# First four units of a fused scan and MLP kernel: memsets moved back, a clip moved forward, weights converted at other places, another rule for warming products

## The chip, the cores and the metric

The kernel runs on one core of one Trainium2 chip. The metric is the time of one execution on the device in microseconds (us); several runs are taken and their median is given. A trace of one profiled execution goes with it; its times count from the start of its span.

## What is computed

Three stages follow each other. The first is a state-space scan over x (4 batches, 8 heads, 768 steps, 32 wide) with decays a and matrices B and C of 16 states:

```python
log_a = np.log(np.clip(a, 1e-06, 1.0))
for c in range(nc):                    # chunks of the sequence
    L = np.exp(cum[..., :, None] - cum[..., None, :]) * causal
    M = np.einsum('bhin,bhjn->bhij', Cc, Bc) * L
    y = M @ xc + (Cc @ state) * np.exp(cum)
    state = decay_full * state + sum_j(Bc x xc * decay_from_j)
```

The second takes its result as 3072 tokens of 256 numbers, norms them (`x / sqrt(mean(x*x) + 1e-6) * g`) and runs a gated MLP, `silu(xn @ w_gate) * (xn @ w_val) @ w_out`, 1536 wide. The third is `softplus(x @ w_in) @ w_out`, 2048 wide.

## The kernel before

The scan is cut into 24 units of 128 steps of one batch, and the MLPs into six blocks of four units (512 tokens). Units 0 to 3 form block 0, and nothing of the MLPs can run until they are done and normed. Matrix products are made in three passes of fp32r parts: every operand has a high part (a copy on ScalarE, ACT) and a low part (a subtraction on VectorE, DVE).

**A unit.** For units 0 to 3 TensorE (PE) spreads the decays over 128 partitions (`spread0`, `spread1`, L539 to L551) into PSUM, DVE runs a scan over each half (L552), PE multiplies C by B (`scores`, L577 to L587), DVE multiplies scores by decays (`decay`, L601), POOL or DVE scales B (`scale`, L572), and PE makes the unit's products (L613 to L626). Then ACT squares them (L648) and applies the gains (L651), PE sums the squares (`msum`), ACT takes the mean (L727), POOL the root (`power`, L729), PE spreads it (`rspread`), DVE multiplies (`norm`, L750), and high and low parts are made (`high` on ACT L347, `low` on POOL or DVE L354). PE has four PSUM buffers `p`, one of which belongs to the warming products, and two each of `a` and `t`.

**The start.** The decays of units 0 to 3 come in by two small loads into `st`, are clipped on DVE (`clip4`, L894), copied on ACT (L897), subtracted on DVE (L898), and only then can be spread. POOL clears `st` first, later the tiles `zz` (used by the weights) and `cz` (used from unit 8 on). The decays of all units are loaded into a tile `s`, clipped on DVE (`clip_all`, L902 and a memset, L903) and stored to `a_clip` in DRAM (L910), from which the units behind the fourth read them back; POOL clips the tile once more in place (L909), DVE makes running products of it (L931) and they too are stored.

**A weight.** Each of 34 chunks (512 KB) is loaded into one of three buffers `wr` (L428), then ACT converts 16 bits of it into `zz` (L436), DVE shifts and joins (L439), ACT makes the high part (L443) and DVE the low part (L445). For the first two chunks `FIRST` gives the places of these four steps.

**The order.** All instructions are issued in an order that a planner makes when the kernel is built. An operation recorded while `plan.now` has a value is a lead operation: on its engine, lead operations run in the order of these values, which `LEAD` and `FIRST` give for the first four units (0 is the first scan; negative values around `LOADS` belong to the start). A first pass of the planner places the lead operations alone and notes a time for each, `due`. The second pass places all: other operations go in between, those of lower `rank` first, where they don't push the next lead operation of their engine more than `SLIP` (100 ns) past its due time. The planner reckons 300 ns for a hand-off between engines, a clock of PE of its own (`clock`), and lets POOL hold the port that it shares with DVE's operations marked `port`.

**Warming products.** Up to 200 products of a constant (`filler`, 512 columns each, rank `SPARE`) serve to keep PE at work; what is not placed when the last lead operation is out is dropped. Before the change they go by the rule of the other operations: the whole of one has to end by the next lead operation's due time of the first pass, plus `SLIP`.

Of the kernel before, what the change touches and what calls it, by code (L numbers as in the profile page):

```python
# [36 lines left out]

LOADS = -50.0

FIRST = [(12.5, 14.8, 17.0, 17.3), (13.0, 15.4, 17.8, 20.4)]  # L40

LEAD = dict(
    spread0=(-0.6, 0.0, 2.6, 6.1), spread1=(-0.4, 1.5, 3.7, 9.6), scores=(-0.2, 4.9, 8.4, 12.1), products=(6.0, 9.5, 13.5, 15.0),
    msum=(7.9, 11.1, 15.3, 16.9), rspread=(10.6, 13.2, 17.9, 18.9),
    scan0=(0.0, 2.28, 5.75, 9.3), scan1=(1.14, 4.6, 8.1, 11.95), decay0=(3.4, 6.9, 10.4, 13.3), decay1=(4.0, 7.5, 11.0, 13.9),
    scale=(2.6, 6.0, 9.6, 13.1), norm=(11.6, 14.5, 18.3, 19.4),
    square=(7.3, 10.8, 14.5, 16.3), gains=(7.6, 11.1, 14.9, 16.6), mean=(8.7, 11.9, 16.8, 17.65), state=(8.8, 12.0, 17.7, 19.0),
    power=(8.9, 12.2, 17.3, 18.3), high=(12.2, 15.1, 18.9, 19.9), low=(12.9, 15.6, 18.8, 20.0))

W_LEAD, T0, U_LEAD, U_GAP, U_GAP0, U1, U1_GAP, B_LEAD, EPI = 50, 50, 115, 8, 4, 10, 14, 50, 40  # L50
# [1 line left out]
SLIP = 100  # L52
# [25 lines left out]
class Plan:  # L78
# [58 lines left out]
    def run(self, which, due, times, warm=False):  # L137

        ops, seq = self.ops, self.seq
# [35 lines left out]
        cand = {e: set() for e in engines}  # L175
        free = {e: 0.0 for e in engines}
        port = 0.0
        queues, served = ("sp", "actq"), 0.0
        ticks = {}

        def enter(i):
            for e in ops[i][0]:
                cand[e].add(i)

        def start(i, e):
            t = max(ready[i], free[e])
            if e == "dve" and ops[i][0][e][2:]:
                t = max(t, port)
            for key, b in news[i]:
                head = b.turn < first[key] + need[i, key]  # L190
                if len(slots[key]) < need[i, key] + (0 if head else ANY_ORDER.get(key[1], 99)):
                    return None
                t = max(t, sorted(slots[key])[need[i, key] - 1])
            return t
# [5 lines left out]
        spare = {i for i in chosen if ops[i][1] >= SPARE and i not in seq}  # L200
        todo = len(chosen) - len(spare)
        while todo:
            best = None
            if spare and all(at[e] == len(lane[e]) for e in engines):
                for i in spare:
                    for e in engines:
                        cand[e].discard(i)
                    for b in uses[i]:
                        b.left -= 1
                        if not b.left:  # L210
                            slots[b.pool, b.tag].append(b.rel)
                spare = set()
            for e in engines:
                able = []
                turn = lane[e][at[e]] if at[e] < len(lane[e]) else None
                for i in cand[e]:
                    if i in seq and i != turn:
                        continue
                    t = start(i, e)
                    if t is None or i not in seq and turn is not None and t + (475 if e in queues else ops[i][0][e][0]) > due[turn] + SLIP:  # L220
                        continue
                    able.append((t, i not in seq, ops[i][1], i))
                while able:
                    t, _, rank, i = least = min(able)
                    if best is not None and t >= best[0]:
                        break
                    end = t + ops[i][0][e][0]

                    later = False
                    for e2, way in ops[i][0].items():  # L230
                        if e2 != e:
                            ns, t2 = way[0], start(i, e2)
                            t2 += sum(ops[j][0][e2][0] for j in cand[e2]
                                      if len(ops[j][0]) == 1 and ops[j][1] < rank and ready[j] <= t2)
                            later = later or t2 + ns < end
                    if not later:
                        best = (t, e, i)
                        break
                    able.remove(least)
            if best is None:  # L240
                raise RuntimeError("no operation can run")
            t, e, i = best
            ns, fn, *shared = ops[i][0][e]
            times[i] = t
            for e2 in ops[i][0]:
                cand[e2].discard(i)
            if i in seq:
                at[e] += 1
            end = t + ns
            if e == "pe" and not warm:  # L250
                end = self.clock(t, ns, ops[i][4], ticks)
            if e in queues:

                served = max(t + 1100, served) + ns
                end = served + DMA_LAT
                free[e] = t + 475
            else:
                free[e] = end
                if e == "pool":
                    port = end  # L260
            order.append(fn)
            todo -= i not in spare
            spare.discard(i)
            for key, b in news[i]:
                slots[key].remove(min(slots[key]))
                taken[key].add(b.turn)
                while first[key] in taken[key]:
                    first[key] += 1
            for b in uses[i]:
                b.left -= 1  # L270
                b.rel = max(b.rel, end + self.latency)
                if not b.left:
                    slots[b.pool, b.tag].append(b.rel)
            for j, data in succ[i]:
                if data:
                    ready[j] = max(ready[j], end + (20 if list(ops[j][0]) == [e] else self.latency))
                left[j] -= 1
                if not left[j]:
                    enter(j)
# [4 lines left out]
def tile_ssd_then_swiglu_then_softplus_mlp(  # L284
# [11 lines left out]
    act, dve, pool, pe = nc.scalar, nc.vector, nc.gpsimd, nc.tensor  # L296
    plan = Plan(LAT)
# [29 lines left out]
    def dve_ns(n, fast=False):  # L327
        return 68 + n * (0.52 if fast else 1.04)
# [4 lines left out]
    def pool_ns(n):  # L333
        return 150 + n * 2.1

    def DVE(n, rank, fn, r=(), w=(), fast=False, port=True, ns=None):
        plan.op({"dve": (ns or dve_ns(n, fast), fn) + (("port",) if port else ())}, rank, r, w)
# [4 lines left out]
    def POOL(n, rank, fn, r=(), w=()):  # L342
        plan.op({"pool": (pool_ns(n), fn, "port")}, rank, r, w)
# [14 lines left out]
    def LOAD(kb, rank, fn, w, r=()):  # L358
        plan.op({"sp": (kb * DMA_NS, fn)}, rank, r, w)
# [11 lines left out]
    mean = const.tile([P, 64], F32, name="mean")[:, 0:1]  # L371
    sel = small[:, 4 * SPREAD:8 * SPREAD].bitcast(F32R)
    cz = [const.tile([P, 4, 2, P], F32, name=f"cz{i}") for i in range(2)]
    zz = [const.tile([P, 4 * P], F32, name=f"zz{i}") for i in range(2)]
# [24 lines left out]
    seq = [(1, t) for t in range(HEAD)] + [(2, t) for t in range(HEAD)]  # L399
# [15 lines left out]
    def weight(c):  # L415
# [12 lines left out]
        LOAD(512, -60 + c if c < N_W else rank, lambda: nc.sync.dma_start(out=raw().bitcast(U16)[:, 1:16 * P + 1], in_=w[c].bitcast(U16)), [raw])  # L428
        first = FIRST[c] if c < len(FIRST) else [None] * 4
        n = 2 * KD * P  # L430
# [435 lines left out]
    with tc.manual_schedule():  # L866
# [8 lines left out]
        def a_view(t):  # L875
            return t.rearrange("u o (h g i) -> (u o h) g i", g=2, i=P)
# [27 lines left out]
        p_sb = buf("s", [NU * 4, 2, P], F32, N_S)  # L904
        plan.now = LOADS + 4.5
        LOAD(96, -97.5, lambda: nc.sync.dma_start(out=p_sb(), in_=a_view(ab)), [p_sb])
        plan.now = None
        DVE(384, -52, clip_all, [p_sb], [a_sb])
        POOL(256, -50, lambda: pool.tensor_scalar(out=p_sb(), in0=p_sb(), scalar1=1.0, scalar2=1e-6, op0=ALU.min, op1=ALU.max), [p_sb], [p_sb])  # L909
        LOAD(96, -50, lambda: nc.sync.dma_start(out=a_view(a_clip), in_=a_sb()), ["a_clip"], [a_sb])  # L910
        plan.now = LOADS + 3.5
        LOAD(128, -98.5, lambda: nc.sync.dma_start(out=cst_sb[:, 0:DM + 1 + KD], in_=cst), ["cst", "g"])
        plan.now = LOADS - 10
        DVE(1, -104, lambda: dve.memset(mean, 1.0 / DM), (), ["mean"])
        DVE(1, -101, lambda: dve.memset(mhalf, -0.5), (), ["mhalf"])
        plan.now = LOADS + 10
        for i in range(2):
            POOL(500, -103, lambda i=i: pool.memset(zz[i], 0.0), (), [("zz", i)])
        plan.now = None
        for i in range(2):  # L920
            POOL(500, -1 + i, lambda i=i: pool.memset(cz[i], 0.0), (), [("zero", i)])

        wp.append(pbuf('p', [P, 4 * P]))
        for i in range(FILL):
# [109 lines left out]
```

## Time and profile before

| | us |
|---|---|
| median of 3 runs | 637.34 (637.11 to 638.5) |
| the profiled execution | 637.81 |
| its span | 636.0 |
| PE busy | 627.1 (99% of the span) |
| DVE busy | 355.2 (56%) |
| ACT busy | 313.8 (49%) |
| POOL busy | 25.3 (4%) |

The span lies 1.81 us under the time of the same execution. [...] A timeline merges neighbouring instructions of one kind: each line gives the start, the time to the end of the last of them, and their number.

### The profile page before, as it was taken

Reading aid. Unit: us, or ns where it says so; the run is one execution under the profiler, and the core shown is the slowest. Engines: PE = TensorE matmul, PEld = TensorE weight load, DVE = VectorE, ACT = ScalarE, POOL = GpSimd, SP = SyncE. Lnnn points to the kernel's source line nnn. Section 1 sums busy time; section 2 is a strip of 40 time slices with the busy share of each in tenths; the row PEclk is TensorE's granted clock in tenths of the full one; section 3 lists DMA queues with packets and bytes.
Section 4 is the critical chain, followed back from the end, with each engine's and each line's share of the span. In section 5 each row is a group of like instructions: output and inputs, shape, how many; then the busy total and the mean of one; then the engine's idle time right before and its main releaser. Section 6 shows DMA issues by size and latency. Waiting matters only on the chain.

```text
span 636.0 us, 8696 instructions
## 1 busy us (share of the span) xinstructions
PE 627.1 (99%) x3348; PEld 516.9 (81%) x3348; DVE 355.2 (56%) x561; ACT 313.8 (49%) x559; POOL 25.3 (4%) x41
## 2 busy tenths in 40 slices
PE   8999999999999999999999999999999999999997
PEld 6787788888888888888888888888888888888885
DVE  7689997788683235695333669656333433322222
ACT  2565665678565445344644344556433332544543
POOL 3201100001000000000000000000000000000000
PEclk8599999999999999999999999999999999999999
DMA  6097658466611006011345531500000000000000
GB/s 202 35 275 247 208 196 270 166 228 227 215 56 54 1 5 204 33 55 38 115 155 174 177 121 37 160 0 1 34 1 1 0 1 1 1 0 1 33 2 33
DMA packets 33433, 59.81 MB, mean 94 GB/s; under 512 B 3120, under 2 KB 14960, under 8 KB 33392
## 3 DMA queue, kind: packets, MB, share of 16 engines
q1 hardware_dynamic: 33248, 59.00, 28.0%
q8 instruction: 26, 0.43, 0.3%
q10 hardware_dynamic: 144, 0.26, 0.1%
q14 instruction: 15, 0.12, 0.1%
HBM read 47.52 MB, written 11.73 MB: 93 GB/s over the span
## 4 chain that ended last, share of the span: by engine, by line
PE 91%; DVE 6%; issue 1%; ACT 1%; POOL 0%; DVEq 0%; ACTq 0%; POOLq 0%
PE p L316 50%; PE t L316 35%; PE a L316 5%; DVE ab L552 2%; DVE ab L601 1%; DVE wr L439 1%; DVE s L801 1%; DVE hw L354 1%; ACT zz L436 0%; ACT xxl L651 0%; DVE wol L445 0%; POOL rs L729 0%; DVE wgl L445 0%; ACT xxh L648 0%; ACT hw L347 0%
## 5 line engine op out<-in xcount | busy, mean ns | idle before, releaser
L354 DVE TENSOR_TENSOR hw<-s,hw 128x512 fp32r<-128x512 f32 x164 | 113.2, 691 | 161.8 <-ACT hw L347 160.9
L347 ACT ACTIVATE hw<-s 128x512 fp32r<-128x512 f32 x164 | 103.4, 632 | 103.1 <-DVE s L801 76.7
L316 PE MATMUL t<-hw,wph 128*128 128x512 f32 x384 | 119.3, 391 | 0.0
L813 ACT ACTIVATE s<-p 128x512 f32<-128x512 f32 x96 | 57.2, 599 | 89.8 <-PE p L316 87.3
L801 DVE TENSOR_TENSOR s<-s,p 128x512 f32<-128x512 f32 x72 | 49.2, 683 | 68.1 <-PE p L316 57.7
L316 PE MATMUL t<-hw,woh 128*128 128x512 f32 x272 | 85.5, 394 | 1.7 <-DVE hw L354 1.7
L316 PEld LDWEIGHTS t<-hw,wph 128*128 128x128 f32 x384 | 71.6, 188 | 16.1 <-ACT hw L347 0.6
L316 PE MATMUL p<-xxh,wih 128*128 128x512 f32 x192 | 74.9, 390 | 0.0
L316 PE MATMUL t<-hw,wpl 128*128 128x512 f32 x192 | 74.8, 389 | 0.0
L316 PE MATMUL p<-xxl,wih 128*128 128x512 f32 x192 | 74.8, 389 | 0.0
L316 PE MATMUL p<-xxh,wil 128*128 128x512 f32 x192 | 74.7, 389 | 0.0
L797 ACT ACTIVATE s<-p 128x512 f32<-128x512 f32 x72 | 43.0, 597 | 55.1 <-PE p L316 54.3
L316 PEld LDWEIGHTS t<-hw,woh 128*128 128x128 f32 x272 | 50.5, 188 | 13.7 <-DVE hw L354 2.7
L316 PE MATMUL p<-xxh,wgh 128*128 128x512 f32 x144 | 56.6, 393 | 0.0
L316 PE MATMUL p<-xxh,wvh 128*128 128x512 f32 x144 | 56.4, 392 | 0.0
L316 PE MATMUL p<-xxl,wgh 128*128 128x512 f32 x144 | 56.2, 390 | 0.0
L316 PE MATMUL p<-xxl,wvh 128*128 128x512 f32 x144 | 56.1, 390 | 0.0
L316 PE MATMUL p<-xxh,wgl 128*128 128x512 f32 x144 | 56.1, 389 | 0.0
L316 PE MATMUL p<-xxh,wvl 128*128 128x512 f32 x144 | 56.0, 389 | 0.0
L316 PE MATMUL t<-hw,wol 128*128 128x512 f32 x136 | 53.0, 389 | 0.0
L552 DVE TENSOR_TENSOR_SCAN ab<-ab,ident 128x512 f32<-128x512 f32 x40 | 48.8, 1227 | 0.0
L316 PEld LDWEIGHTS p<-xxh,wih 128*128 128x128 f32 x192 | 36.0, 188 | 7.7 <-issue 0.2
(131 smaller groups left out, 768.1 us busy)
## 6 DMA issues: line engine op xcount, KB each, us to landing
wr<-in_w SPq DMA_DIRECT2D x34, 512.0 KB
ab<-a_clip SPq DMA_DIRECT2D x20, 512.0 KB
parts<-wr SPq DMA_DIRECT2D x16, 512.0 KB
xc<-in_xc SPq DMA_DIRECT2D x20, 256.0 KB
st<-parts SPq DMA_DIRECT2D x16, 256.0 KB
cz<-parts SPq DMA_DIRECT2D x32, 128.0 KB
out_y<-s SPq DMA_DIRECT2D x11, 256.0 KB
wr<-in_bc SPq DMA_DIRECT2D x8, 256.0 KB
```

Of the source, the lines that this page charges most:

```text
L316: pe.matmul(out=o, lhsT=l, rhs=r, start=start, stop=stop, skip_group_check=True)
L347: ways = {"act": (act_ns(n), lambda: act.activation(out=out(), in_=in_(), func=ACTF.Copy)), "dve": (dve_ns(n, sbuf), lambda: dve.tensor_co ...
L354: return lambda: eng.tensor_tensor(out=out(), in0=in_(), in1=f32(hi()), op=ALU.subtract)
L439: DVE(n, rank, lambda: dve.scalar_tensor_tensor(out=mid(), in0=mid(), scalar=13, in1=z.bitcast(I32), op0=ALU.logical_shift_right, op1=ALU. ...
L552: DVE(512, rank[0], lambda t=t, d=d: dve.tensor_tensor_scan(out=t(), data0=d(), data1=ident4, initial=0.0, op0=ALU.mult, op1=ALU.add), dk ...
L601: dve.tensor_tensor(out=m, in0=m, in1=g, op=ALU.mult)
L797: ACT(n, rank - EPI, lambda: act.activation(out=s()[:, 0:n], in_=ps[0]()[:, 0:n], func=ACTF.Silu), [ps[0]], [s, "table"] if new_table else ...
L801: DVE(n, rank - EPI, lambda: dve.tensor_tensor(out=s()[:, 0:n], in0=s()[:, 0:n], in1=ps[1]()[:, 0:n], op=ALU.mult), [s, ps[1]], [s], port= ...
L813: ACT(n, rank - EPI, lambda: act.activation(out=s()[:, 0:n], in_=hp()[:, 0:n], func=ACTF.Softplus), [hp], [s, "table"] if new_table and f ...
```

## The change

It moves the clearing of `zz` on POOL behind unit 0's scale and that of `cz` behind unit 1's, with other durations for the planner (they were 500 elements' worth each). It makes the clip of all units' decays a lead operation between the second scan of unit 1 and the first of unit 2, the POOL clip and the store likewise. The first two chunks' conversions get earlier places on ACT and DVE: the two `zz` conversions ahead of unit 0's high part, the high part of the first ahead of unit 1's, that of the second ahead of unit 3's square. On PE unit 2's row sums come ahead of unit 3's products, and unit 0's root spread ahead of unit 3's second spread. And a warming product may now go wherever the next lead operation is not ready to be placed; where it is, the product has to end before that operation's start in this pass.

```diff
-FIRST = [(12.5, 14.8, 17.0, 17.3), (13.0, 15.4, 17.8, 20.4)]
+FIRST = [(12.05, 14.4, 15.0, 17.3), (12.1, 15.2, 16.2, 20.4)]
...
-    spread0=(-0.6, 0.0, 2.6, 6.1), spread1=(-0.4, 1.5, 3.7, 9.6), scores=(-0.2, 4.9, 8.4, 12.1), products=(6.0, 9.5, 13.5, 15.0),
-    msum=(7.9, 11.1, 15.3, 16.9), rspread=(10.6, 13.2, 17.9, 18.9),
+    spread0=(-0.6, 0.0, 2.6, 6.1), spread1=(-0.4, 1.5, 3.7, 9.6), scores=(-0.2, 4.9, 8.4, 12.1), products=(6.0, 9.5, 13.5, 15.3),
+    msum=(7.9, 11.1, 15.2, 16.9), rspread=(9.55, 13.2, 17.3, 18.9),
...
-    square=(7.3, 10.8, 14.5, 16.3), gains=(7.6, 11.1, 14.9, 16.6), mean=(8.7, 11.9, 16.8, 17.65), state=(8.8, 12.0, 17.7, 19.0),
+    square=(7.3, 10.8, 14.5, 16.3), gains=(7.6, 11.1, 14.9, 16.6), mean=(8.7, 11.9, 16.15, 17.65), state=(8.8, 12.0, 17.7, 19.0),
...
                     t = start(i, e)
-                    if t is None or i not in seq and turn is not None and t + (475 if e in queues else ops[i][0][e][0]) > due[turn] + SLIP:
+                    if t is None:
                         continue
+                    if i not in seq and turn is not None:
+                        until = due[turn] + SLIP
+                        if i in spare:
+                            until = start(turn, e) if turn in cand[e] else None
+                        if until is not None and t + (475 if e in queues else ops[i][0][e][0]) > until:
+                            continue
...
-        plan.now = None
+        plan.now = 5.74
         DVE(384, -52, clip_all, [p_sb], [a_sb])
+        plan.now = 6.2
         POOL(256, -50, lambda: pool.tensor_scalar(out=p_sb(), in0=p_sb(), scalar1=1.0, scalar2=1e-6, op0=ALU.min, op1=ALU.max), [p_sb], [p_sb])
+        plan.now = 5.8
         LOAD(96, -50, lambda: nc.sync.dma_start(out=a_view(a_clip), in_=a_sb()), ["a_clip"], [a_sb])
...
-        plan.now = LOADS + 10
+        plan.now = 2.7
         for i in range(2):
-            POOL(500, -103, lambda i=i: pool.memset(zz[i], 0.0), (), [("zz", i)])
-        plan.now = None
+            POOL(180, -103, lambda i=i: pool.memset(zz[i], 0.0), (), [("zz", i)])
+        plan.now = 6.1
         for i in range(2):
-            POOL(500, -1 + i, lambda i=i: pool.memset(cz[i], 0.0), (), [("zero", i)])
+            POOL(370, -1 + i, lambda i=i: pool.memset(cz[i], 0.0), (), [("zero", i)])
```

## Rows read from the trace of the kernel before

**Rows 1.** Busy time by stretch: PE, PEld, DVE, ACT, POOL, granted clock, DMA share, GB/s
```profile
50.00:60.00 10.00, 9.46 (x80) 7.01 (x73) 9.86 (x16) 6.93 (x15) 1.83 (x2) 1.00 0.61 197
...
80.00:90.00 10.00, 9.62 (x51) 7.95 (x51) 9.66 (x24) 5.89 (x11) 0.00 (x0) 1.00 0.50 176
...
sum 600.00, PE 598.32 PEld 493.69 DVE 333.23 ACT 302.81 POOL 16.03; mean PE 9.97 PEld 8.23 DVE 5.55 ACT 5.05 POOL 0.27
```

**Rows 2.** Timeline of PE to 60 us: start, length, line, tiles, count, idle before
```profile
0.92 5.33 PE L316 MATMUL p<-mean 128*128 128x512 f32 x13 [0.92 <-DVE small L915]
6.09 0.63 PE L316 MATMUL p<-st,small 128*128 128x256 f32 x4
...
24.04 1.08 PE L316 MATMUL t<-xxl,s 128*32 128x128 f32 x16
25.05 1.87 PE L316 MATMUL p<-mean,xxh 128*128 128x1 f32 x8
27.02 0.79 PE L316 MATMUL p<-ident,rs 128*128 128x128 f32 x2
28.70 0.80 PE L316 MATMUL p<-ident,rs 128*128 128x128 f32 x2 [0.89 <-POOL rs L729]
29.15 3.33 PE L316 MATMUL p<-mean 128*128 128x512 f32 x7
32.28 0.63 PE L316 MATMUL p<-xxh,wgh 128*128 128x512 f32 x1
...
49.55 0.62 PE L316 MATMUL a<-ab,xc 128*32 128x128 f32 x16
```

**Rows 3.** Timeline of DVE to 45 us
```profile
3.49 1.30 DVE L894 TENSOR_SCALAR st<-st 64x256 f32<-64x256 f32 x1 [2.59 <-DMA st<-in_ab]
...
5.44 0.41 DVE L898 TENSOR_TENSOR st<-st 16x256 fp32r<-16x256 f32 x1 [0.53 <-ACT st L897]
...
17.18 1.28 DVE L601 TENSOR_TENSOR xxh<-xxh,a 128x512 f32<-128x512 f32 x2 [0.36 <-PE a L316]
19.50 0.42 DVE L750 TENSOR_TENSOR xxl<-xxl,p 128x256 f32<-128x256 f32 x1 [1.03 <-PE p L316]
...
22.15 1.28 DVE L601 TENSOR_TENSOR xxl<-xxl,a 128x512 f32<-128x512 f32 x2 [0.30 <-PE a L316]
...
23.68 1.28 DVE L439 SCALAR_TENSOR_TENSOR wr<-wr,zz 128x512 int32<-128x512 int32 x2
26.92 0.69 DVE L445 SCALAR_TENSOR_TENSOR wgl<-wr,wgh 128x512 fp32r<-128x512 f32 x1 [1.96 <-ACT wgh L443]
...
30.44 0.43 DVE L354 TENSOR_TENSOR xxl<-xxl,xxh 128x256 fp32r<-128x256 f32 x1 [0.48 <-ACT xxh L347]
...
31.38 0.28 DVE L902 TENSOR_SCALAR Sm<-s 96x256 f32<-96x256 f32 x1
31.73 0.06 DVE L903 MEMSET Sm<- 96x2 f32 x1
```

**Rows 4.** Timeline of POOL to 45 us
```profile
3.70 0.95 POOL L921 MEMSET cz<- 128x1024 f32 x1
```

**Rows 5.** Busy time by single microseconds, columns as in rows 1
```profile
9.00:10.00 1.00, 0.41 (x2) 0.21 (x2) 1.00 (x2) 0.00 (x0) 0.35 (x1) 1.00 0.56 191
...
13.00:14.00 1.00, 1.00 (x14) 0.62 (x6) 1.00 (x3) 0.38 (x2) 0.00 (x0) 0.50 0.95 299
...
20.00:21.00 1.00, 1.00 (x9) 0.98 (x11) 1.00 (x1) 0.80 (x4) 0.55 (x2) 0.50 0.00 0
...
32.00:33.00 1.00, 1.00 (x4) 0.77 (x3) 1.00 (x2) 0.70 (x2) 0.15 (x1) 0.59 0.33 86
```

**Rows 6.** Timeline of SP's queue to 60 us
```profile
8.64 23.23 SPq L428 DMA_DIRECT2D wr<-in_w  x5
31.96 0.38 SPq L910 DMA_DIRECT2D a_clip<-Sm  x1
```

**Rows 7.** Timeline of ACT to 45 us
```profile
28.02 0.66 ACT L443 ACTIVATE wvh<-wr 128x512 fp32r<-128x512 f32 x1
```

## The prediction

> **What bounds the kernel now.** I read the stretches of ten microseconds first. From 30 us to the end TensorE (PE) is busy for 598.32 of 600.00 us, and its few gaps, 1.68 us in all, lie between 50 and 90 us, where VectorE (DVE) is busy 97 to 99% of the time [rows 1]. So the time is: when the first product of the MLP starts, plus a fixed amount of matrix work, plus those gaps. The first such product starts at 32.28 us [rows 2]. The change touches only what lies before it. Second I read PE's timeline up to that product, third DVE's, because the first four units alternate between the two, and last the granted clock by microsecond. The reader is to see three wastes.
>
> First, the clip of the first four units' a (L894) takes 1.30 us on DVE, beside a POOL memset of cz from 3.70 us, while the same operation on a larger tile later (L902) takes 0.28 us [rows 3, 4]. [...] DVE then waits for PE: 0.36, 1.03 and 0.30 us before its steps at 17.18, 19.50 and 22.15 us [rows 3]. Third, seven warming products stand in PE's queue from 29.15 us; the last operand (the low part of unit 3's rows) is done at 30.44 + 0.43 = 30.87 us, the main product starts 1.41 us later [rows 2, 3].
>
> **The start chain.** With the two zz memsets behind unit 0's scale and the cz memsets behind unit 1's, nothing of POOL stands beside L894: 1.30 becomes 0.28, so the operand of the first spread is ready at 5.44 + 0.41 - 1.02 = 4.83 instead of 5.85 us [rows 3]. But PE's queue holds 13 warming products ahead of that spread, from 0.92 to 6.09 us, 0.40 us each on average [rows 2]. How many remain is the planner's doing; its due time for the spread contains the memsets as an occupied port, so it will lay fewer. Bounds: none fewer, 0; all that are in the way, 1.02 us, where the operand decides. I take the middle, -0.5.
>
> **The clip among the scans.** L902 and the memset behind it cost DVE 0.28 + 0.06 us [rows 3], now in a stretch where DVE never rests: +0.34. Its input was asked for before the weights, whose issues begin at 8.64 us [rows 6], and it comes at about 11.5 us, so I expect no wait. The a_clip store goes into SP's queue behind three weight loads instead of five; the fourth load stands behind it, but that waits for the first weight's last conversion, far later, so the store delays nothing. It moves from 31.96 us [rows 6] to about 12.5, and the next units' loads, which read a_clip, can use a stretch in which the DMA engines now move nothing (0 GB/s at 20 us [rows 5]). The two cz memsets, 0.95 us each [rows 4], and POOL's own clip lie in front of unit 0's root on POOL, which could come up to half a microsecond late; what it feeds, DVE's first norm step, is late in DVE's order, so I cost it at nothing; without that cover it is 0.5.
>
> How dear is the clip if POOL writes SBUF beside it? The row says 1.30 instead of 0.28 (L894), +1.02 on DVE's chain; scale of unit 1 and the cz memsets run right behind the scan that the clip follows, so this can happen. [...] I keep +0.34 (DVE is already at work on the clip when unit 1's scale is released), and +1.36 as the far end.
>
> **The clock.** No row shows these narrow products with 512-wide warming products in every gap between them. The nearest rows: with gaps the clock fell; with narrow products alone it stayed at half; seven warming products in a row brought it to 1.00 within 33 us (0.59 on average from 32 to 33) [rows 5, 2]. The gaps on PE in the first units are there to be filled, and under the new rule a warming product goes in whenever the next planned step is not ready. I take full clock throughout; the other end is half clock throughout (a rival below). At full clock DVE's three waits go: -1.69. The 16 products of unit 3 take 0.62 instead of 1.08 us (the like row at full clock is at 49.55 [rows 2]): -0.46. Row sums at 25.05 (8 products, units 2 and 3) and the spread at 27.02 fill PE for 2.76 us before unit 3's mean [rows 2]; now unit 2's sums are ahead of unit 3's products, and what is left is a square on ScalarE (ACT) and four products, some 0.9: -1.85. The last spread at 28.70 (0.45 until the next product starts) halves: -0.2.
>
> The rows show PE busy at 1.00 and the clock at 0.50 for a dozen microseconds [rows 5]. [...]
>
> **A new wait on ACT.** The second weight's high part (0.66 us [rows 7]) now stands ahead of unit 3's square, and it waits for the shift on DVE. Behind unit 3's last product with the scores DVE does both shifts (1.28 us [rows 3]) and a norm step, some 1.65 in all; 2.4 us later the square starts, where it could have started about 1.25 us after. Waiting behind it: unit 3's square, gains, row sums, mean, root, spread. +1.15 (bounds 0 and 1.3).
>
> **The warming products at the end.** They wasted 1.41 us. At full clock each takes half as long; the planner reckons 0.3 us for each hand-off between engines, which is much, so some waste stays. Bounds 0 and 1.4; I take 0.6, that is -0.8.
>
> **Sum up to the main products.** Unit 3's last DVE step ends at 22.15 + 1.28 = 23.43; -0.5 +0.34 -1.69 makes 21.6. From there to the last operand it was 30.87 - 23.43 = 7.44; -0.46 -1.85 -0.2 +1.15 makes 6.1, so 27.7; +0.6 makes 28.3 instead of 32.28: -4.0. The first main products then run at full clock (0.63 us for the first [rows 2]): -0.25.
>
> **After it.** DVE is nearly the bound between 42 and 90 us, and must be earlier by as much. Its steps of unit 3 are 1.85 earlier, and it idled before, for instance 1.96 us before 26.92 [rows 3]; more of it lay before 42 us, for weights and units not yet loaded, which now come sooner. Bounds: all 1.68 us of gaps go; or the shift beyond 1.85 is given back, +2.2. I take +0.15. Total -4.1. The profiled execution is 637.81 us (span 636.0), the median 637.34, 0.47 less; I apply the sum to the median: 633.2 us.
>
> **Rivals.** (1) Slower: the clock falls all the same, and warming products at half rate lengthen the one queue that then bounds the stage. The gains left are 0.5 at the start less 0.34 for the clip, and up to 1.41 at the end, 1.6 at most. A warming product at half rate is 0.43 to 0.45 us (3.13 us for seven [rows 2]); the fourth one laid in this stage beyond what before had undoes the gain. Ten, about three per unit, cost 4.4: +2.8, 640.1 us. For it: half clock beside busy 1.00. Against: its own remedy, since more 512-wide products are what brought the clock back. Chance 0.18. (2) The clock holds for the first two units and falls in the third or fourth: about half of the 4.2 us of clock terms, and a few slow warming products (1 us) are lost, gain 1.0: 636.3 us, within the noise at either side. Chance 0.12. (3) DVE gives back what lies beyond its own shift: gaps between 50 and 90 us grow by 2.2, gain 2.0: 635.3 us. For it: DVE 97 to 99% busy there. Against: idle DVE before 42 us, and weights and loads that are sooner. Chance 0.15. (4) The memsets do not leave the clip's side but meet the second one, +1.02, and the first spread is not earlier, +0.5: gain 2.6, 634.7 us; this only narrows the forecast and I count it there. Forecast with it: 0.55.
>
> **How the numbers follow.** What a measurement of this kernel can tell is 0.2%, 1.3 us, so faster means below 636.1. The forecast and the third rival lie there: 0.70. The second: 0.12 for the same. The first: 0.18 slower. The forecast's own range is 631.2 (gaps of 1.68 gone and 0.2 less waste at the end) to 635.5; the whole range reaches to the second rival's slow side, 637.9, and leaves out the first.
>
> **What would show it.** Right: L894 at about 0.3 us; the first scan near 6.0; granted clock 1.00 from 12 us on; DVE without waits between 6 and 21 us; the first main product between 27.5 and 29; gaps of under 2 us behind it. Wrong: clock 0.50 between 13 and 28 with warming products at 0.43 us between the narrow ones; L902 at over 1 us; the square of unit 3 later than 24; or new gaps with DVE as releaser between 45 and 90 us.

## The result and the profile after

The changed kernel takes 630.75 us (median of 4 runs, 630.32 to 631.63) against 637.71 of the kernel before beside it: a ratio of 0.9892, with a 95% interval of 0.9875 to 0.9909, or 7.0 us less. A second series on another chip gave 630.90 us and 0.9883 (0.9868 to 0.9898). The direction was forecast; the size was not: 4.1 us were expected, and the range ended at 631.2. The span fell from 636.0 to 628.5 us.

PE's timeline up to the first main products, which answers to [rows 2], and the one wait of PE behind them:

```profile
0.92 4.65 PE L322 MATMUL p<-mean 128*128 128x512 f32 x11 [0.92 <-DVE small L923]
5.41 0.63 PE L322 MATMUL p<-st,small 128*128 128x256 f32 x4
...
23.56 0.60 PE L322 MATMUL p<-mean,xxh 128*128 128x1 f32 x4
24.35 0.49 PE L322 MATMUL p<-ident,rs 128*128 128x128 f32 x2 [0.19 <-POOL rs L735]
...
25.99 0.38 PE L322 MATMUL p<-ident,rs 128*128 128x128 f32 x2
26.30 1.16 PE L322 MATMUL a<-hw 16*128 16x128 f32 x16
27.39 1.14 PE L322 MATMUL p<-mean 128*128 128x512 f32 x4
28.37 0.40 PE L322 MATMUL p<-xxh,wgh 128*128 128x512 f32 x1
...
35.19 0.39 PE L322 MATMUL t<-hw,woh 128*128 128x512 f32 x1
36.13 0.50 PE L322 MATMUL t<-hw,woh 128*128 128x512 f32 x1 [0.55 <-DVE hw L360]
```

The first main product starts at 28.37 instead of 32.28 us. The line to notice is the one at 26.30: the scores of unit 4, which belong to the second block, are now ahead of the main products, in time that warming products would have had. In the kernel before they stood behind and cost PE 1.09 us (44.93 to 46.02):

```profile
44.93 1.16 PE L316 MATMUL a<-hw 16*128 16x128 f32 x16
```

DVE's timeline, for [rows 3]:

```profile
3.58 0.28 DVE L900 TENSOR_SCALAR st<-st 64x256 f32<-64x256 f32 x1 [2.68 <-DMA st<-in_ab]
...
5.84 3.45 DVE L558 TENSOR_TENSOR_SCAN ab<-p,ident 128x512 f32<-128x512 f32 x3 [0.92 <-PE p L322]
...
11.52 0.26 DVE L908 TENSOR_SCALAR Sm<-s 96x256 f32<-96x256 f32 x1
11.83 1.22 DVE L558 TENSOR_TENSOR_SCAN xxh<-p,ident 128x512 f32<-128x512 f32 x1
...
19.67 1.29 DVE L607 TENSOR_TENSOR xxl<-xxl,a 128x512 f32<-128x512 f32 x2
...
27.37 0.42 DVE L360 TENSOR_TENSOR xxl<-xxl,xxh 128x256 fp32r<-128x256 f32 x1 [0.54 <-ACT xxh L353]
```

The first clip is down to 0.28 us. The other clip (11.52) displaces the next scan by 0.31. From 5.84 to 24 us no line of DVE has an idle time of any size in front; before there were 0.36, 1.03 and 0.30 us.

Busy time by stretch, for [rows 5] and [rows 1] (PE, PEld, DVE, ACT, POOL, granted clock, DMA share, GB/s; the sum is over seven stretches from 30 to 100 us):

```profile
9.00:10.00 1.00, 1.00 (x7) 0.92 (x6) 1.00 (x3) 0.00 (x0) 0.60 (x2) 1.00 0.90 254
...
13.00:14.00 1.00, 1.00 (x9) 0.92 (x7) 1.00 (x3) 0.61 (x3) 0.91 (x2) 1.00 0.88 274
...
20.00:21.00 1.00, 1.00 (x14) 0.76 (x5) 1.00 (x3) 0.70 (x3) 0.56 (x1) 1.00 0.98 311
...
sum 70.00, PE 69.45 PEld 56.19 DVE 67.20 ACT 45.65 POOL 5.95; mean PE 9.92 PEld 8.03 DVE 9.60 ACT 6.52 POOL 0.85
```

The granted clock is a share of PE's full rate: where it reads 1.00, products 512 columns wide follow each other every 0.23 us (28.61 to 28.84 here), and where it reads 0.50, every 0.43 us (32.28 to 32.71 in the kernel before). The clock column is 1.00 throughout, and the microsecond at 20, in which no byte moved before, carries 311 GB/s. SP's queue shows what is moved, for [rows 6], and then the same load in the kernel before:

```profile
11.94 0.33 SPq L918 DMA_DIRECT2D a_clip<-Sm  x1
16.07 0.33 SPq L517 DMA_DIRECT2D ab<-a_clip  x1
```

```profile
35.60 0.38 SPq L511 DMA_DIRECT2D ab<-a_clip  x1
```

Units 4 and 5 are loaded at 16.07 and 17.97 us; before, the same loads stood at 35.60 and 38.25.

**Where 7.5 us of span come from.** The first main product is 3.91 us earlier. Unit 4's 1.09 us of scores lie ahead of it. The main products run at full clock at once: the fourth starts 0.70 us behind the first instead of 0.96, another 0.26. The three waits of PE behind it (two of them here, of the kernel before)

```profile
52.78 0.50 PE L316 MATMUL t<-hw,woh 128*128 128x512 f32 x1
53.81 0.50 PE L316 MATMUL t<-hw,woh 128*128 128x512 f32 x1 [0.54 <-DVE hw L354]
...
64.63 0.39 PE L316 MATMUL t<-hw,woh 128*128 128x512 f32 x1
65.79 0.50 PE L316 MATMUL t<-hw,woh 128*128 128x512 f32 x1 [0.77 <-DVE hw L354]
```

cost more than their idle time says. Such products follow each other every 0.23 us; here 1.03 and 1.16 us pass, so the waits cost 0.80 and 0.93, and the third, at 85 us, 0.63: 2.36 in all, against 0.71 for the one that is left (35.19 to 36.13). That is 1.65. The four make 6.9; the remaining 0.6 us lie spread over the rest and are not placed.

### The profile page after: what moved, and what is told of

The parts are those of the page before. It is cut to its first block, busy times and chain, and to the rows that moved or that the text cites. A ratio compares the mean times of both kernels' runs of the same rounds, so it can differ in the third digit from the quotient of the medians.

```text
span 628.5 us, 8771 instructions
## 1 busy us (share of the span) xinstructions
PE 622.8 (99%) x3378; PEld 514.8 (82%) x3378; DVE 354.0 (56%) x561; ACT 315.1 (50%) x559; POOL 27.2 (4%) x41
## 4 chain that ended last, share of the span: by engine, by line
PE 98%; DVE 1%; ACT 0%; POOL 0%; issue 0%; ACTq 0%
PE p L322 54%; PE t L322 37%; PE a L322 7%; POOL xxl L360 0%; ACT zz L442 0%; DVE wr L445 0%; DVE s L354 0%; DVE xxl L607 0%; POOL rs L735 0%; DVE hw L360 0%; DVE s L807 0%; ACT xxh L353 0%; ACT wgh L449 0%; DVE xc L578 0%; ACT rs L733 0%
```

## The experiments

Every run below stands against the kernel before on its own chip (medians there 637.95 to 638.42 us), so ratios are compared.

| run | what it is | us | ratio (95%) |
|---|---|---|---|
| a1 | changed, old rule for warming products | 636.02 | 0.9982 (0.9968 to 0.9995) |
| a2 | changed, clip not led | 633.93 | 0.9930 (0.9915 to 0.9945) |
| a3 | changed, memsets early | 632.07 | 0.9903 (0.9887 to 0.9920) |
| a4 | changed, old FIRST and LEAD | 629.19 | 0.9860 (0.9845 to 0.9874) |
| b1 | before, new rule alone | 633.76 | 0.9927 (0.9912 to 0.9942) |
| b2 | before, clip led alone | 636.22 | 0.9963 (0.9949 to 0.9976) |
| c1 | changed, two tiles for roots | 631.31 | 0.9886 (0.9869 to 0.9902) |
| d1 | a4 and c1 | 630.92 | 0.9884 (0.9869 to 0.9899) |
| h1 | the changed kernel again | 630.90 | 0.9883 (0.9868 to 0.9898) |
| e1 | changed, old FIRST alone | 630.04 | 0.9876 (0.9859 to 0.9892) |
| e2 | changed, old LEAD alone | 631.04 | 0.9886 (0.9869 to 0.9902) |
| f1 | a4, fewer warming products at the end | 629.09 | 0.9855 (0.9841 to 0.9870) |

### a1: the old rule for warming products

```diff
-                    if i not in seq and turn is not None:
-                        until = due[turn] + SLIP
-                        ...
+                    if t is None or i not in seq and turn is not None and t + (...) > due[turn] + SLIP:
+                        continue
```

> The changed kernel with the old rule for warming products, all else changed. Theory (the new products hold the clock): the granted clock falls to 0.50 near 12.4 us and stays there into the first main products, TensorE bounds the first four units again, the first main product comes near 31 to 32 us, and the time is 633.5 to 635.5 us. Rival (the places and the memsets carry the gain, the products only fill idle time): under 1 us slower than the changed kernel, 631 to 631.7, with the first main product before 29.5 us.

636.02 us, with runs from 635.92 to 637.78. Most of the gain is gone. The stretches (columns as above) and PE's first main products:

```profile
12.00:13.00 1.00, 1.00 (x25) 0.58 (x17) 1.00 (x1) 0.00 (x0) 1.00 (x3) 0.50 1.02 299
...
33.00:34.00 1.00, 1.00 (x4) 0.71 (x4) 1.00 (x4) 1.00 (x2) 0.00 (x0) 0.50 0.77 279
```

```profile
32.08 0.80 PE L316 MATMUL p<-xxh,wgh 128*128 128x512 f32 x1
```

The clock falls as it did before, and the main products start at 32.08 us at half rate. They go on at half rate until past 35 us (the clock is 0.73 on average from 30 to 40 us); unit 4's scores stand directly ahead of them, and no warming product does. So the first theory holds, a little beyond its numbers: places, memsets and clip without the rule bring 1.1 us by the ratio (2.0 by the medians).

### a2: the clip of all units not led

```diff
-        plan.now = 5.74
+        plan.now = None
         DVE(384, -52, clip_all, [p_sb], [a_sb])
-        plan.now = 6.2
         POOL(256, -50, ...)
-        plan.now = 5.8
         LOAD(96, -50, ... a_clip ...)
```

> The changed kernel with the clip of all units' decays, POOL's clip and the store to a_clip not led any more, as before. Theory (the early clip fetches the next units' data in an idle stretch of the DMA engines, and that closed the gaps behind 50 us and brought unit 4's scores ahead of the first main product): DVE's early chain gets 0.3 us shorter, but 1 to 2 us of TensorE gaps come back behind the first main product and unit 4's scores lie behind it; 632.0 to 633.5 us. Rival (the gaps closed because VectorE as a whole was earlier): within 0.7 us of the changed kernel, gaps under 0.8 us.

633.93 us, above the theory's range; by the ratios 2.4 us are lost. SP's queue, PE's start and the sum of the seven stretches:

```profile
27.03 0.33 SPq L517 DMA_DIRECT2D ab<-a_clip  x1
```

```profile
26.21 2.87 PE L322 MATMUL p<-mean 128*128 128x512 f32 x12
28.92 0.40 PE L322 MATMUL p<-xxh,wgh 128*128 128x512 f32 x1
```

```profile
sum 70.00, PE 68.50 PEld 54.23 DVE 66.22 ACT 43.20 POOL 4.47; mean PE 9.79 PEld 7.75 DVE 9.46 ACT 6.17 POOL 0.64
```

Unit 4 is loaded 11 us later, so its scores are not there when PE has time: behind the last root spread twelve warming products stand where the scores and four of them stood in the changed kernel. The gaps between 30 and 100 us are back to 1.50 us from 0.55. Both halves of the theory are to be seen.

### a3: the memsets at their old places

```diff
-        plan.now = 2.7
+        plan.now = LOADS + 10
-            POOL(180, -103, ... zz ...)
+            POOL(500, -103, ... zz ...)
-        plan.now = 6.1
+        plan.now = None
-            POOL(370, -1 + i, ... cz ...)
+            POOL(500, -1 + i, ... cz ...)
```

> The changed kernel with the zz and cz memsets at their old places and with their old planned durations. Theory (POOL's memset beside the clip of the first four units holds up VectorE, and the planner lays more warming products ahead of the first spread): that clip takes 1.0 to 1.3 us instead of 0.28, 16 warming products stand in front, the first scan starts 0.8 to 1.3 us later than 5.84 us, and nothing catches up: 631.5 to 632.2 us. Rival (the start is hidden by later waits): within 0.3 us of the changed kernel.

632.07 us, 0.9903 against 0.9892: the medians differ by 1.3 us as expected, the ratios by 0.7 us, and the intervals overlap. DVE's timeline:

```profile
3.52 1.31 DVE L900 TENSOR_SCALAR st<-st 64x256 f32<-64x256 f32 x1 [2.63 <-DMA st<-in_ab]
...
6.81 3.45 DVE L558 TENSOR_TENSOR_SCAN ab<-p,ident 128x512 f32<-128x512 f32 x3 [0.91 <-DMA xc<-in_xc]
```

The clip takes 1.31 us again, sixteen warming products stand in front, and the first scan starts 0.97 us later. The main products start at 29.47, 1.10 later.

### a4: the old places of the conversions, row sums, products and roots

```diff
-FIRST = [(12.05, 14.4, 15.0, 17.3), (12.1, 15.2, 16.2, 20.4)]
+FIRST = [(12.5, 14.8, 17.0, 17.3), (13.0, 15.4, 17.8, 20.4)]
...
+    products=(..., 15.0), msum=(..., 15.3, ...), rspread=(10.6, ..., 17.9, ...), mean=(..., 16.8, ...)
```

> The changed kernel with the old FIRST and LEAD, that is the old places of the first weights' conversions, unit 2's mean and row sums, unit 3's products and the root spreads. Theory (these moves shift little, since unit 3's square no longer waits for the second weight's high part while the weights come later): the first main product between 27.8 and 29.2 us, time 630.3 to 632.0. Rival (the earlier weights are what lets the main products start early): the first main product 1.5 us or more later, 632.3 or more.

629.19 us: lower than either bound, and 1.6 us under the changed kernel. This part of the change costs time. PE's first main product, and its sum over the seven stretches:

```profile
27.89 0.40 PE L322 MATMUL p<-xxh,wgh 128*128 128x512 f32 x1
```

```profile
sum 70.00, PE 70.00 PEld 56.79 DVE 67.50 ACT 46.63 POOL 3.46; mean PE 10.00 PEld 8.11 DVE 9.64 ACT 6.66 POOL 0.49
```

The main products start 0.48 us earlier, and no gap is left where the changed kernel has 0.55 (0.71 from start to start); together that is 1.2 of the 1.3 us between the spans. Unit 3's square starts at 22.02 us instead of 23.13, yet the last operand comes only 0.31 us earlier (27.48 instead of 27.79).

### b1 and b2: one part alone on the kernel before

b1 and b2, each on the kernel before and with nothing else:

```diff
-                    if t is None or i not in seq and turn is not None and t + (...) > due[turn] + SLIP:
+                    if t is None:
...
+                        if i in spare:
+                            until = start(turn, e) if turn in cand[e] else None
```

```diff
-        plan.now = None
+        plan.now = 5.74
         DVE(384, -52, clip_all, [p_sb], [a_sb])
+        plan.now = 6.2
         POOL(256, -50, ...)
+        plan.now = 5.8
         LOAD(96, -50, ... a_clip ...)
```

> The kernel before with the new rule for warming products alone. Theory (the rule by itself holds the clock, and that is worth most of the gain): granted clock 1.00 from 6 us on, VectorE without waits for TensorE between the first scan and unit 3's last product with the scores, first main product between 28.5 and 30.5 us, but gaps of 1 to 2 us behind it; 632.5 to 635.0 us. Rival (it needs the other parts beside it): over 635.5 us.

> The kernel before with the clip of all units' decays, POOL's clip and the store to a_clip led among the early scans, and nothing else. Theory (the clip fetches the next units early, which closes gaps and lets unit 4's scores fill time ahead of the main products, whatever the clock): the clock still falls to 0.50, gaps behind the first main product under 1 us, 635.0 to 637.0 us. Rival (at half clock TensorE has no time to spare ahead of the main products, so there is no gain): 637.2 to 638.8 us.

b1 takes 633.76 us, b2 636.22; both theories stand (b1's main products start at 27.97, earlier than its bounds). In b1 PE's main products start early and its gaps remain; in b2 the gaps vanish, though the clock is at half until past 37 us (0.64 on average from 30 to 40 us). PE's first main product and the sum of the seven stretches, of b1 and then of b2:

```profile
27.97 0.40 PE L322 MATMUL p<-xxh,wgh 128*128 128x512 f32 x1
```

```profile
sum 70.00, PE 67.91 PEld 53.71 DVE 66.55 ACT 41.98 POOL 4.55; mean PE 9.70 PEld 7.67 DVE 9.51 ACT 6.00 POOL 0.65
```

```profile
29.81 2.08 PE L316 MATMUL a<-hw 16*128 16x128 f32 x16
...
32.83 0.63 PE L316 MATMUL p<-xxh,wgh 128*128 128x512 f32 x1
```

```profile
sum 70.00, PE 70.00 PEld 56.80 DVE 66.91 ACT 44.70 POOL 4.75; mean PE 10.00 PEld 8.11 DVE 9.56 ACT 6.39 POOL 0.68
```

So each part has an effect without the other. The rule brings the start forward; the early clip gives unit 4's scores a place ahead (29.81 in b2) and closes the gaps behind. At half clock the scores have a price: two warming products instead of seven stand ahead of the main products, and ten of these start 0.43 us after each other where the kernel before has one. At 0.23 us each that is about 1.7 us, an estimate from these rows, and b2's gain is what is left after it. That the one brings the other is argued, not tested. In b1 the gaps are 2.09 us although DVE's last step of the scores there (19.84 + 1.28 us) ends within 0.2 us of the changed kernel's, which is against the idea that gaps close because DVE as a whole is earlier.

### c1 and d1: two tiles for the roots

```diff
-            rs = buf("rs", [P, 64], F32)
+            rs = buf("rs", [P, 32], F32, 2)
```

In the changed kernel unit 3's mean on ACT waits although its row sums, issued at 23.56, are done by 24.16 us:

```profile
23.13 0.37 ACT L654 ACTIVATE xxh<-t 128x256 f32<-128x256 f32 x1
...
24.88 0.17 ACT L733 ACTIVATE rs<-p 128x1 f32<-128x1 f32 x1 [0.85 <-PE p L322]
```

It starts when unit 2's root spread (24.35 + 0.49) ends: both units use the one tile `rs`.

> The changed kernel with two buffers instead of one for the small tile of the roots (rs), half as wide each. Theory (unit 3's mean waits for unit 2's root spread, since both use the one tile): the mean comes by 24.3 us instead of 24.88, unit 3's root spread by 25.5 instead of 25.99, the first main product by about 27.9, 630.0 to 630.5 us. Rival (the mean waits for its own row sums): no change within 0.3 us.

> The changed kernel with the old FIRST and LEAD and with two buffers for the roots. Theory (both waits ahead of unit 3's norm step are gone): 0.2 to 0.8 us under the run with the old places alone (629.19), 628.4 to 629.0 us. Rival (ScalarE's own queue now sets unit 3's mean): the same as with the old places alone within 0.2 us.

c1 takes 631.31 us (0.9886): no gain. ACT's mean, PE behind it, and DVE's last operand:

```profile
24.82 0.17 ACT L733 ACTIVATE rs<-p 128x1 f32<-128x1 f32 x1 [0.25 <-PE p L322]
```

```profile
24.12 0.61 PE L322 MATMUL p<-mean,xxh 128*128 128x1 f32 x4
...
26.33 0.38 PE L322 MATMUL p<-ident,rs 128*128 128x128 f32 x2
...
27.74 1.36 PE L322 MATMUL p<-mean 128*128 128x512 f32 x5
```

```profile
27.72 0.42 DVE L360 TENSOR_TENSOR xxl<-xxl,xxh 128x256 fp32r<-128x256 f32 x1 [0.54 <-ACT xxh L353]
```

The wait is gone: the mean follows its own row sums by 0.09 us (24.73 to 24.82) instead of 0.72. (This execution's first units ran some 0.56 us later, so its times are compared by steps.) From unit 3's row sums to its root spread it was 2.43 us (23.56 to 25.99) and is 2.21; to the main product it was 4.81 and is 4.81. Five warming products, not four, now stand at the end. The last operand is ready 4.02 us behind the row sums (24.12 to 28.14) instead of 4.23, and the main product, at 28.93, starts 0.79 us behind it instead of 0.58: the queue that the planner fills by its own times took the gain. d1 is worse than a4 (0.9884 against 0.9860, on different chips): its trace has two waits of PE, at 50 and 88 us, that a4 has not, 0.46 and 0.71 us from start to start. They make 1.2 of the 1.8 us between the two spans. The order of the rest changed with the edit; why these waits came was not followed up.

### h1, e1, e2: which of the places cost time

h1 is the changed kernel itself; e1 takes only the old `FIRST`, e2 only the old four entries of `LEAD`:

```diff
-FIRST = [(12.05, 14.4, 15.0, 17.3), (12.1, 15.2, 16.2, 20.4)]
+FIRST = [(12.5, 14.8, 17.0, 17.3), (13.0, 15.4, 17.8, 20.4)]
```

```diff
-    products=(..., 15.3), msum=(..., 15.2, ...), rspread=(9.55, ..., 17.3, ...), mean=(..., 16.15, ...)
+    products=(..., 15.0), msum=(..., 15.3, ...), rspread=(10.6, ..., 17.9, ...), mean=(..., 16.8, ...)
```

> The changed kernel itself, for a comparison on one chip with the next three. Both theories: 630.3 to 631.7 us, first main product near 28.4 us.

> The changed kernel with the old FIRST alone (the first two weights' conversions where they were, the new LEAD kept). Theory (the second weight's high part ahead of unit 3's square is what the new places cost): the square of unit 3 starts near 22.0 us instead of 23.13, unit 3's root spread comes about 0.3 us earlier, the gap behind the first main product goes, and the time is that of the old places, 0.8 to 1.8 us under the changed kernel. Rival (the new LEAD costs it, unit 2's row sums ahead of unit 3's products): within 0.5 us of the changed kernel.

> The changed kernel with the old LEAD alone (the new FIRST kept). Theory (FIRST costs it): within 0.5 us of the changed kernel, unit 3's square still near 23.1 us. Rival (LEAD costs it): 0.8 to 1.8 us under the changed kernel.

e2 is the changed kernel within 0.2 us. e1 lies 0.9 us under it by the medians, with overlapping intervals: unclear. Neither alone is sure to bring a4's 1.6. PE's gap behind the main products is gone in e1 (busy 70.00 of 70.00 us) and stays in e2 (69.45). The other half of e1's theory did not come: unit 3's square starts at 22.66, its root spread at 25.99 as in the changed kernel, and eleven warming products hold the main products until 28.62. So the new `LEAD` costs nothing beside the new `FIRST`, and with both old the gain is there; how it divides stays open.

### f1: two warming products fewer at the end

```diff
+                    if i in spare and turn is None and tail >= 7:
+                        continue
...
+            tail += i in spare and at["pe"] == len(lane["pe"])
```

> The changed kernel with the old FIRST and LEAD, and at most seven warming products behind the last lead operation of TensorE, where nine stood. Theory (the plan lays more of them than the real hand-offs need, and they hold up the main product): the first main product 0.3 to 0.45 us earlier than 27.89, and the time 0.2 to 0.5 us under that of the old places alone, 628.6 to 629.1. Rival (TensorE then waits for its operands just as long): no difference.

629.09 us (0.9855), not to be told from a4 (0.9860). The main product does come earlier:

```profile
27.68 0.39 PE L326 MATMUL p<-xxh,wgh 128*128 128x512 f32 x1
```

0.21 us by the clock of the two traces, and 0.44 from unit 3's root spread (25.93 against 25.70 in a4), for this execution began later. But a wait of 0.29 us, from start to start, appears at 33.4 us where a4 has none. On one chip with h1, f1 is 1.8 us faster (628.67 to 629.38 against 630.40 to 631.07, no overlap): the old places are better, and these two kernels, a4 and f1, are the fastest of the study.

## Why the prediction was wrong, step by step

All the signs that it named for being right came, the gaps of under 2 us behind the first main product among them. What failed is the price of what comes after that product's start.

**The start chain** was right in kind: L894 fell to 0.28, 11 of 13 warming products are left, the spread comes 0.68 us earlier (0.5 was taken, the middle of two bounds). a3, where 16 stand in front, returns it. The 0.68 is one execution of each: among the profiles with eleven in front the spread starts anywhere from 5.38 us (a4) to 5.77 (a2).

**The clip among the scans** costs 0.31 us as costed (0.34). The worse end, a collision with POOL, did not come: the clip took 0.26.

**The clock** held, as the forecast took it: 1.00 in every microsecond from 6 to 40 us, where the kernel before has 0.50 from 13 to 32; the first rival fell with it. No row of the kernel before shows that it would: full clock throughout was the author's estimate. The rows now show narrow products and 512-wide warming products in turn at 1.00, with PE busy 1.00 in those shown. Busy time alone does not tell the two kernels apart: before, PE is busy 1.00 from 13 to 26 us as well, at 0.50, and 0.92, 0.79 and 0.29 in the three microseconds from 26. In a1, where a single warming product stands between the first spread and 12 us, PE is 0.85, 0.50 and 0.60 busy in the three microseconds from 7, and the clock is 0.50 from 12. What sets the clock the runs do not show. DVE's three waits are gone as summed.

**The new wait on ACT** is there: unit 3's square starts at 23.13, 2.17 us behind the last of the scores' products on DVE (2.4 was said). It was not the only one: unit 3's mean then waited for unit 2's root spread, by the shared tile, which the prediction did not see. The same wait is in the kernel before, where row sums are done by 26.92 us, the spread by 27.81, and the mean starts at 27.85:

```profile
27.85 0.17 ACT L727 ACTIVATE rs<-p 128x1 f32<-128x1 f32 x1 [0.96 <-PE p L316]
```

The prediction read it as PE being full. From unit 3's last product to this mean it was 2.80 us (25.05 to 27.85) and is 2.63 (22.25 to 24.88), where the sum's -1.85 and +1.15 make 2.10. In front of the spread in the changed kernel stood POOL's subtraction, here the second, and beside it on DVE the low part of a weight:

```profile
19.83 0.73 POOL L360 TENSOR_TENSOR xxl<-xxl,xxh 128x256 fp32r<-128x256 f32 x1 [0.42 <-ACT xxh L353]
22.69 0.98 POOL L360 TENSOR_TENSOR xxl<-xxl,xxh 128x256 fp32r<-128x256 f32 x1 [2.13 <-ACT rs L733]
```

```profile
22.41 0.69 DVE L451 SCALAR_TENSOR_TENSOR wgl<-wr,wgh 128x512 fp32r<-128x512 f32 x1
```

The subtraction took 0.98 us there and 0.73 where the first ran, beside DVE's scores step at 19.67. In c1 the second took 0.97, again beside the low part (22.97 to 23.65 us). Whether the one slows the other was not tried.

From DVE's last step to the last operand it was 6.8 us, not 6.1 (20.96 to 27.79). DVE itself ended 0.6 earlier than summed (20.96 against 21.6), 0.34 of it because its scale of unit 3 took 0.42 instead of 0.76 us, which the sum left out. The two errors cancel, and that is luck.

**The warming products at the end** waste 0.58 us (27.79 to 28.37); 0.6 was taken. The start of the main products, 28.3 by the sum, is 28.37.

**After it** is the step that failed. "I take +0.15" stood, with a gain of 1.68 us as the best bound, where the runs show a gain of 2.74: 1.65 in waits and 1.09 in scores that moved ahead. Two things were missing. The prediction saw that the early clip lets the next units load in an idle stretch, and gave that no price beyond DVE's idle time; that PE's own work of unit 4 could take the place of warming products was not thought of. b2 (2.2 us from the clip alone) and a2 (its loss) show that the early clip brings this time. And the bound of 1.68 us was read from idle times, while from start to start the same waits cost 2.36. With 1.09 more and the waits so counted, the low end of the range would have been near 629.4. The third rival, DVE giving time back, had the sign wrong.

**By parts**, in ratios against before: the rule alone 0.7%, the clip alone 0.4%, the memsets about 0.1%, and the new places cost about 0.2 to 0.3%. The parts don't have to add up: without the rule, b2's first main products run at half rate, 0.43 us apart.

## What to carry to other kernels

When an order is made by a planner, an early load may do two things, as here: close waits later (2.36 us of them, against the 0.71 left) and put real work where the planner had filled in idle work (1.09 us of scores); price both. Count a wait of PE from start to start of its products, not by its idle time: the wait left in the changed kernel costs 0.71 us where 0.55 is called idle. And filler work is laid by the planner's clock, so a wait removed ahead of it may be handed back by one more filler, as the two root tiles show: five warming products instead of four, and 4.81 us from row sums to main product with either.

## What the runs showed of the hardware that was not expected

The time at which PE's first products go from one every 0.43 us to a faster pace differs between executions. Thirteen warming products stand in front of the first spread both in the kernel before, where it starts at 6.09 us [rows 2], and in b2, where the same 13 last until 6.52:

```profile
0.92 5.77 PE L316 MATMUL p<-mean 128*128 128x512 f32 x13 [0.92 <-DVE small L917]
6.52 0.63 PE L316 MATMUL p<-st,small 128*128 128x256 f32 x4
```

They follow each other every 0.43 us, half rate, up to 5.34 us in the kernel before and 6.20 in b2, while the clock column gives 1.00. In these first microseconds the column does not tell the rate, and profiles of two kernels may differ by some 0.4 us from that alone (6.09 against 6.52 here). With eleven products in front it is the same: the spread starts at 5.38 us in a4, at 5.41 in the changed kernel and at 5.77 in a2.

In b2 the memsets also stand at their early place, yet the first clip takes 0.31 us, not 1.30. This time POOL's memset is the longer one, 1.09 instead of 0.95 us:

```profile
3.72 0.31 DVE L894 TENSOR_SCALAR st<-st 64x256 f32<-64x256 f32 x1 [2.83 <-DMA st<-in_ab]
```

```profile
3.84 1.09 POOL L923 MEMSET cz<- 128x1024 f32 x1
```

In the kernel before, a3 and b1 the clip ends 0.14 us behind that memset (at 4.79 against 4.65 us in the kernel before), as if it had to wait for it. Which of the two starts first by the profile does not settle it, for the clip is ahead in the kernel before (3.49 against 3.70) as in b2. What does, and is worth a microsecond, was not tried.
